# mLSTM with two gated layers on one core: o gates in five pieces, first step's k, q, v ahead of the weights, and a new order for the first third

## The chip, the cores and the metric

The kernel runs on one core of a Trainium2 chip. The metric is the device time of one execution in microseconds (us), the median of several runs; lower is better. The core has TensorE (PE in the rows; its weight loads are PEld), VectorE (DVE), ScalarE (ACT), GpSimd (POOL) and SyncE (SP), which here does nothing but issue loads and stores. Each engine works off its own queue in order and waits on semaphores for the others.

## The reference

```python
def _attn_ref(q, k, v, i_gate, f_gate, o_gate):      # (2, 8, 768, 40), gates without the 40
    for t in range(S):
        m_new = np.maximum(f_gate[:, :, t] + m, i_gate[:, :, t])
        f_stab = np.exp(f_gate[:, :, t] + m - m_new)
        i_stab = np.exp(i_gate[:, :, t] - m_new)
        C = f_stab * C + i_stab * np.einsum('bhd,bhe->bhde', vt, kt)
        n = f_stab * n + i_stab * kt
        h_tilde = np.einsum('bhde,bhe->bhd', C, qt)
        denom = np.maximum(np.abs(np.einsum('bhd,bhd->bh', n, qt)), 1.0)
        y[:, :, t] = sigmoid(o_gate[:, :, t]) * h_tilde / denom

x = y as (1536, 320)
x = (sigmoid(x @ w_gate) * (x @ w_val)) @ w_out      # 320 -> 1536 -> 320
out = ((x @ w_a) * (x @ w_b)) @ w_out2               # 320 -> 1536 -> 320
```

## The kernel before

The recurrence runs in 12 steps of 64 time positions, all 16 heads at once (2 batches, 4 pairs of heads). Within a step it is written with matrices. The layers are cut in 12 blocks of 128 hidden columns each. The weights come as 64-bit floats, are narrowed to 32 bit in the kernel, and each is split into a rounded part and its remainder, since products run in a reduced 32-bit format.

Every piece of work is a task with a name, declared with what it needs and which buffers it takes. The string PLAN lists the tasks in the order in which the kernel issues them; a letter behind a colon picks the engine where there is a choice (V is DVE, G GpSimd, A ACT), and `*n` puts n multiplications by zeros on TensorE ahead of the task. There is no other scheduler: PLAN sets each engine's queue. The names, with s a step, c a block of weights, u a unit:

- loads (SP): `start`, `gl1`, `gl2` the input and forget gates; `cst` constants; `kq`s and `kv`s the keys, queries and values; `og`i the o gates; `w`c weights. Two weight blocks can be held at a time (`wst`, freed by `s2`, `s3`).
- gates: `ga`, `gb`, `gd`, `gc` on DVE, `ge` on ACT, once for each of three pieces of time.
- a step: `pr` or `pl` prepares the operands of the exponents; `E0`, `E1` form the exponents on TensorE, `X0`, `X1` take exp on ACT; `S` is q times k, `P` the product of S and exp on DVE; `k` weighs the keys, `ST` sums the new state on TensorE and `st` copies it on ACT; `O` is the output, `N` and `M` scale and normalise it with the sigmoid of the o gate; `D` copies some columns twice, `T` transposes, `xh` and `xl` split the tokens.
- `sg`i: the sigmoid of load `og`i on ACT, for several steps at once. `yz`, `yi` set up the three buffers Y that hold values and state.
- weights: `na` on ACT, `nb`, `ns`, `nc`, `nd` narrow; `s1` on ACT, `s2`, `s3` split. `s1` of block 3 or 4 waits for the sigmoids whose o gates lie in that block's buffer.
- a unit (one weight block, two or four groups of 128 tokens): `ma`, `mb` the two products of 8 matmuls, `ga_` the activations, `gp`, `gm` the product, `gh_`, `gl_` its split, `mm` the second product, `ev` its evacuation. The first 24 units, the head, take two groups (256 tokens) and form their sigmoid from exp and tanh (L537 to L539), so that ACT needs one table for them and for `X`. The o gates' sigmoid (L339) needs another table. ACT loads a table when the next function is not in the one it has.

In the head, units are put between the steps of the recurrence: unit 0 and 1 work on steps 0 and 1, 2 and 3 on steps 2 and 3, and so on. A head unit takes one of two banks for `ma` and `mb` together, freed by `gp`. Behind the head come units of 512 tokens.

Of the kernel before, what the change touches and what calls it, by code (L numbers as in the profile page):

```python
# [68 lines left out]
pr1:V nb0 yz0 kv0 E01*1 E10*6 gl2 gc1 yz2 ns0 yz1 kv1 X01 X10 ga2 pr2:V yi0:A nc0 k10:V kq0 yi2:A k00:V E11*4
X11 S0 pr3:V w1 kq1 E02 kq2 nd0:V E12 P10 P00 yi1:A k01:G kv2 ST0 st0 na1 X02 og2 S1*10 X12 k11:G k12:G og1  # L70
kq3 gb2 gd2 O0 kv3 ST1 P11 P01 S2*2 pr4:V sg0 nb1 E03 s10 N0 O1*2 P02 P12 st1 s30:G k02:G kq4 ST2 sg2 N1 s20:V
w2 E13 ns1 sg1 M0:G M1:V X03 nc1 k03:G D1 X13 k13:G O2*1 S3 P03 E04 P13 nd1:V E14 D0 kv4 X04 T0*1 X14 T1 st2
xh0 N2 S4 ST3 xl0 pr5:G kq5 P14 xh1 kv5 xl1 O3 s11 s31:G s21:V P04 E15 ma0 N3 M2:V na2 mb0 k04:V ge2 ma1 M3:V
ga_0 mb1 X15 S5 gp0 D3 k14:G st3 nb2 gm0 D2 T2 T3 ga_1 xh2 ns2 gc2 ST4 gh_0 gl_0:G nc2 xh3 O4 st4 kq6 xl2 xl3
nd2:V w3 E05 X05 ma2 mb2 s12 gp1 gm1 pl3 ga_2 ma3 P15 P05 gh_1 k05:G na3 mb3 s22:V gl_1:V s32:V mm0 mm1 kq7
gp2 ma4 mb4 E06 E07 w4 gm2 ga_3 ev0.0:A ev0.1:A nb3 ns3 nc3 nd3:V X06 gh_2 k15:G X07 N4 kv6 S6 gp3 gm3 kv7 E16
s13 P06 ST5 gl_2:G X16 P16 gh_3 gl_3:V O5 pl4 ga_4 S7 st5 E17 mm2 s23:V s33:G gp4 gm4 N5 mm3 X17 ma5 mb5 na4
M5:V k06:G ma6 P07 gh_4 nb4 gl_4:G mb6 O6 ev1.3:A ga_5 P17 ns4 M4:V ev1.2:A k16:V ST6 gp5 gm5 nc4 ma7 D4 T4
ga_6 D5 T5 gh_5 q17:V gp6 gm6 gl_5:G mm4 xh4 xl4 mb7 xh5 xl5 mm5 ga_7 gh_6 nd4:G gp7 ev2.0 N6 s14 k07:G E08
X08 gl_6:G kq8 k17:V gm7 ma8 M6:V st6 w5 mb8 E18 X18 gh_7 ma9 kv8 gl_7:G E19 mb9 ga_8 q18:G ev2.1 mm6 mm7  # L80
q07:V O7 na5 kq9 gp8 ST7 S8 gm8 ga_9 ma10 mb10 ev3.3 ev3.2 N7 M7:V q08:G kv9 D7 nb5 gp9 ma11 gm9 gh_8 X19 E09
P18 gh_9 gl_9:V kv10 mb11 gl_8:G ga_10 gp10 mm8 st7 pl5 k18:G X09 D6 P08 T6 gm10 gh_10 T7 ns5 xh7 xh6 nc5
k08:G mm9 kq10 k19:V ga_11 xl6 O8 gp11 xl7 ST8 gm11 st8 S9 gl_10:G q19:G nd5:V N8 ma12 mm10 gh_11 E110 X110
mb12 ga_12 ma13 mb13 P09 k09:G s34:V P19 gp12 kq11 s15 gm12 gh_12 gl_11:V ga_13 M8:V ma14 s24:V gp13 D8 q09:G
E010 X010 O9 N9 M9:V gm13 ST9 mb14 s25:V mm11 gl_12:G ga_14 ev4.4:A ma15 gp14 gm14 D9 ev4.5:V gh_13 T8 xh8 xl8
T9 mb15 gl_13:G xh9 xl9 mm12 E111 ga_15 X111 q110:V gh_14 w6 ma16 k110:V gl_14:V mm13 mb16 gp15 gm15 ma17
k010:G mm14 na6 nb6 ga_16 E011 ns6 gp16 gh_15 mb17 nc6 ma18 st9 gl_15:V gm16 ga_17 s35:G w7 kv11 X011 nd6:V
gh_16 s16 mm15 gl_16:G S10 q111:G gp17 gm17 gh_17 S11 q010:V P010 ST10 st10 mb18 ga_18 P110 P111 q011:V P011
ev5.6:V gl_17:G O10 ev5.7:A O11 N10 M10:G mm16 mm17 N11 M11:V na7 D10 D11 T10 T11 gp18 gm18 xh10 gh_18 k111:G
nb7 xh11 xl11 xl10 ma19 mb19 ga_19 gp19 gl_18:G mm18 ns7 ma20 gm19 gh_19 mb20 ga_20 gp20 gm20 gh_20 s36:G ma21  # L90
gl_19:G nc7 mb21 ga_21 gp21 gm21 mm19 ma22 gl_20:G s26:V w8 mb22 ev6.8:A nd7:V ma23 ev6.9:A mm20 mb23 ga_22
gp22 gm22 gh_21 gl_21:G ga_23 gp23 ma24 gm23 s17 mm21 gh_22 mb24 gl_22:G gh_23 gl_23:G ga_24 s27:G k011:V mm22
na8 gm24 ma25 ma26 mb25 s37:G mm23 ga_25 w9 gh_24 mb26 ev7.11:V ev7.10:V gl_24 nb8 ga_26 ma27 ns8 nc8 mm24
gm25 nd8:V gh_25 mb27 gm26 gl_25 ga_27 mm25 na9 ma28 gh_26 gl_26 ma29 gm27 gh_27 ga_28 gl_27 mm26 nb9 ga_29
s18 ns9 nc9 mb28 nd9:V mm27 s38:V s19 s28:V ma30 w10 s29:G ev8.1 gm28 gh_28 mb29 gl_28 ev8.0 ga_30 s39:V ma31
w11 gm29 gh_29 gl_29 ma32 ev8.3 ga_31 na10 mb30 mb31 gm30 nb10 ev8.2 ma33 ns10 nc10 mm28 nd10:G mm29 gh_30
na11 gl_30 gm31 mm30 gh_31 ga_32 gl_31 mb32 s110 mm31 s210:G mb33 s310:G ev9.5 ev9.7 gm32 w12 ev9.4 gh_32 ma34
ga_33 gm33 gl_32 mb34 ev9.6 ga_34 nb11 gh_33 ns11 ma35 nc11 nd11:V mm32 s111 ma36 s211:V s311:G mb35 gl_33
ga_35 w13 mm33 gm35 gh_35 na12 gl_35 ma37 gm34 gh_34 mb36 gl_34 ga_36 mb37 ga_37 gm36 mm34 gm37 ma38 mm35 ma39
gh_36 ev10.11 gh_37 gl_36 ev10.9 ga_38 mb39 ev10.8 gl_37 ev10.10 ga_39 nb12 mb38 ns12 mm36 gm38 gm39 nc12 ma40  # L100
nd12:V mb40 na13 mm37 gh_38 nb13 ns13 ma41 gl_38 gh_39 s112 gl_39 nc13 mm38 ga_40 nd13:G ga_41 mm39 s312:G
mb41 ev11.0 gm40 ev11.1 s212:V ma42 gm41 w14 gh_41 mb42 gh_40 gl_40 gl_41 ga_42 ma43 gm42 ev11.2 ev11.3 yt1
# [831 lines left out]
```

## Time and profile before

| | |
|---|---|
| median of 3 runs | 475.48 us (474.09 to 476.25) |
| span of the profiled execution | 478.0 us |
| PE busy | 465.6 us (97%) |
| DVE busy | 295.1 us (62%) |
| ACT busy | 242.5 us (51%) |
| POOL busy | 101.3 us (21%) |
| HBM read, written | 36.71 MB, 1.97 MB |
| multiplications by zeros | 64 |

The profile is of one execution, and its span is 2.5 us above the median of the other runs. The shares are means over a head, in which five engines work on the recurrence and the first units, and a long rest, in which TensorE does the layers. A busy TensorE need not be one at full clock: the granted clock stands in a line or column of its own. The stretch to look at is the first 140 us.

### The profile page before, as it was taken

To read this page: it belongs to the slowest core of one execution; us is meant where nothing else is said; L and a number is where in the kernel's file an instruction comes from. 1 tells how busy PE (TensorE), PEld (TensorE's weight loads), DVE (VectorE), ACT (ScalarE), POOL (GpSimd) and SP (SyncE) were. 2 spreads that over 40 slices of the span, in tenths; PEclk is the share of its full clock that TensorE was granted. 3 is DMA by queue.
4 is the path that set the end of the run, shared out by engine and by line. 5 is a ranking of instruction groups with operands and counts; after the bars stand their busy time and mean duration, and the time that the engine had idled before them with its cause. 6 is when DMAs were issued, how large, how long until landed. Compare 5 with 4: busy or idle time off the path is not lost.

```text
span 478.0 us, 8676 instructions
## 1 busy us (share of the span) xinstructions
PE 465.6 (97%) x3511; PEld 406.2 (85%) x3516; DVE 295.1 (62%) x505; ACT 242.5 (51%) x455; POOL 101.3 (21%) x110
## 2 busy tenths in 40 slices
...
PEclk9969999999999999999999999999999999999998
...
GB/s 226 309 201 240 86 180 224 32 103 183 1 84 84 1 166 0 83 84 1 33 49 84 7 160 0 1 82 138 28 84 82 1 83 1 0 1 20 36 55 55
DMA packets 10454, 39.31 MB, mean 82 GB/s; under 512 B 1840, under 2 KB 3760, under 8 KB 10416
## 3 DMA queue, kind: packets, MB, share of 16 engines
...
q10 hardware_dynamic: 288, 0.33, 0.2%
...
HBM read 36.71 MB, written 1.97 MB: 81 GB/s over the span
## 4 chain that ended last, share of the span: by engine, by line
PE 86%; DVE 6%; ACT 4%; DMA 2%; issue 2%; SPq 0%; DVEq 0%
PE pa L524 30%; PE pb L524 23%; PE acc L531 8%; PE acc L532 8%; PE acc L533 8%; PE o L445 2%; PE sp L416 2%; DMA wst<-in_w_dram 2%; PE st L435 1%; ACT Dt L378 1%; PE e L371 1%; PE t L487 1%; DVE g L556 1%; PE tp L487 1%; PE first L174 1%
## 5 line engine op out<-in xcount | busy, mean ns | idle before, releaser
L524 PE MATMUL pa<-xb,W 128*128 128x512 f32 (+1 forms) x864 | 169.4, 343 | 0.3 <-DVE ge L605 0.3
L524 PEld LDWEIGHTS pa<-xb,W 128*128 128x128 f32 x864 | 136.3, 188 | 18.9 <-DVE ge L605 0.5
L524 PE MATMUL pb<-xb,W 128*128 128x512 f32 x480 | 119.0, 392 | 0.0
L524 PEld LDWEIGHTS pb<-xb,W 128*128 128x128 f32 x480 | 89.0, 188 | 17.9
L560 ACT ACTIVATE gh<-g 128x512 fp32r<-128x512 f32 (+1 forms) x84 | 47.5, 568 | 110.7 <-PE acc L532 55.6
L531 PE MATMUL acc<-W,gh 128*128 128x320 f32 x288 | 89.3, 310 | 0.0
L532 PE MATMUL acc<-W,gh 128*128 128x320 f32 x288 | 88.9, 309 | 0.0
L533 PE MATMUL acc<-W,gl 128*128 128x320 f32 x288 | 88.8, 309 | 0.0
L554 DVE TENSOR_TENSOR g<-g,pb 128x512 f32<-128x512 f32 x60 | 40.9, 685 | 69.7 <-PE pb L524 61.6
L565 DVE TENSOR_TENSOR gl<-g,gh 128x512 fp32r<-128x512 f32 (+1 forms) x66 | 45.5, 694 | 44.0 <-ACT gh L560 43.8
L549 ACT ACTIVATE g<-pa 128x512 f32<-128x512 f32 x60 | 35.6, 595 | 45.8 <-DVE gl L565 38.1
L532 PEld LDWEIGHTS acc<-W,gh 128*128 128x128 f32 x288 | 54.0, 188 | 2.1
L531 PEld LDWEIGHTS acc<-W,gh 128*128 128x128 f32 x288 | 54.0, 188 | 2.0
L533 PEld LDWEIGHTS acc<-W,gl 128*128 128x128 f32 x288 | 54.0, 188 | 0.0
L258 POOL TENSOR_TENSOR W<-wst,W 128x832 fp32r<-128x832 f32 x9 | 19.1, 2124 | 84.5 <-DVE x2tok L639 42.2
L639 DVE SCALAR_TENSOR_TENSOR x2tok<-acc,x2tok 128x320 f32<-128x320 f32 x52 | 23.8, 485 | 19.5 <-PE acc L533 19.5
L242 POOL TENSOR_TENSOR wst<-cva,wst 128x960 int32<-128x960 int32 x7 | 16.9, 2410 | 73.8 <-DVE cva L236 61.1
L218 ACT ACTIVATE cva<-wst 128x960 f32<-128x960 f32 x24 | 25.8, 1077 | 10.6 <-DVE wst L242 8.8
L252 ACT ACTIVATE W<-wst 128x832 fp32r<-128x832 f32 x24 | 23.2, 966 | 11.5 <-DVE wst L242 8.5
L236 DVE SCALAR_TENSOR_TENSOR cva<-wst,cva 128x960 int32<-128x960 int32 x24 | 27.9, 1161 | 0.4
L565 POOL TENSOR_TENSOR gl<-g,gh 128x256 fp32r<-128x256 f32 x18 | 15.7, 876 | 54.7 <-ACT gh L560 47.3
L219 ACT ACTIVATE wst<-wst 128x960 int32<-128x960 uint32 x24 | 26.1, 1087 | 0.0
...
## 6 DMA issues: line engine op xcount, KB each, us to landing
...
cs<-in_cst_dram SPq DMA_DIRECT2D x1, 469.0 KB
rhsE<-V SPq DMA_DIRECT2D x24, 2.0 KB
```

The source lines that it names most:

```text
L218: nc.scalar.activation(cva[0], hi.bitcast(F32), AF.Abs)
L219: nc.scalar.activation(lo, lo.bitcast(U32), AF.Copy, scale=2.0**-29)
L236: nc.vector.scalar_tensor_tensor(ai, hi, -0x40000000, ai, op0=ALU.bitwise_and, op1=ALU.bitwise_or)
L524: nc.tensor.matmul(dst, w[:, w0 : w0 + P], x[:, h, cb], start=(i == 0), stop=(i == 7))
L531: nc.tensor.matmul(a, gh[:, c], wh, start=st, stop=False)
L532: nc.tensor.matmul(a, gh[:, c], wl, start=False, stop=False)
L533: nc.tensor.matmul(a, gl[:, c], wh, start=False, stop=sp)
L549: nc.scalar.activation(t, pa, AF.Copy if l else AF.Sigmoid)
L554: nc.vector.tensor_tensor(t, t, pb, op=ALU.mult)
L560: nc.scalar.activation(gh, g, AF.Copy)
L565: eng.tensor_tensor(gl, g, gh.bitcast(F32), op=ALU.subtract)
L639: nc.vector.scalar_tensor_tensor(dst[:, 0:DM], acc, half, dst[:, 0:DM], op0=ALU.mult, op1=ALU.add)
```

## The change

The o gates come in five loads with five sigmoids (`OGS`) in place of three: steps 0 and 1, 2 and 3, 4 and 5, 6 to 8, 9 to 11. They lie in the buffers of weight blocks 3 and 4, as before. `load_og` finds the place in the buffer by the lowest step in it, since the last piece is now loaded ahead of the fourth. PLAN is rewritten up to `mm21`; from there on it is the same. In the new part 63 multiplications by zeros stand, before 64; the longest row of them is 27, before 37. Engines are changed for some tasks: of the normalisations `M`, GpSimd has 7 in place of 1; of the splits `gl_` DVE has 10 in place of 6; of the head's evacuations DVE has 6 in place of 2, ACT 4 in place of 8.

```diff
-OGS = ((0, 2, 3), (2, 6, 3), (6, 12, 4))
+OGS = ((0, 2, 3), (2, 4, 3), (4, 6, 3), (6, 9, 4), (9, 12, 4))
...
 PLAN = """
-start gl1 cst rhs0:A lhs0:A ga0 ga1 gb0 gd0 ge0 lhs1:A w0 gb1 na0 gc0 gd1 ge1 pr0:V E00*37 og0 X00 rhs1:A
+yz2 start yz0 yz1 gl1 ga0 cst gb0 ga1 lhs0:A gd0 gb1 kv0 kq0 gl2 lhs1:A ge0 rhs0:A gd1 gc0 w0 yi0:A pr0:V
...
-            ogw[k] = wpool.tile([P, 2 * NH + 2 * P], F32, tag=f"W{k}", name=f"og{k}"), s0
+            ogw[k] = wpool.tile([P, 2 * NH + 2 * P], F32, tag=f"W{k}", name=f"og{k}"), min(o[0] for o in OGS if o[2] == k)
```

The loads at the start, on SP's queue. Names end in a running number; kq0 and Y0 are step 0's, wst0 is the first weight block, og3 the o gates in the buffer of block 3. Before:

```order
L678 DMA cs_96<-in_cst_dram 128x938
L211 DMA wst0_135<-in_w1_dram 128x1920
L335 DMA og3_188<-in_ogate_dram 128x640
L324 DMA Y0_103<-in_kv_dram 64x648
L325 DMA Y0_103<-in_kv_dram 64x648
L275 DMA gates2_210<-in_gates_dram 64x2x320
L324 DMA Y1_104<-in_kv_dram 64x648
L325 DMA Y1_104<-in_kv_dram 64x648
L320 DMA kq0_231<-in_kqT_dram 128x1024
L211 DMA wst1_266<-in_w1_dram 128x1920
L320 DMA kq1_268<-in_kqT_dram 128x1024
```

Now:

```order
L679 DMA cs_96<-in_cst_dram 128x938
L325 DMA Y0_103<-in_kv_dram 64x648
L326 DMA Y0_103<-in_kv_dram 64x648
L321 DMA kq0_138<-in_kqT_dram 128x1024
L276 DMA gates2_140<-in_gates_dram 64x2x320
L212 DMA wst0_149<-in_w1_dram 128x1920
L321 DMA kq1_191<-in_kqT_dram 128x1024
L336 DMA og3_199<-in_ogate_dram 128x640
L325 DMA Y1_104<-in_kv_dram 64x648
L326 DMA Y1_104<-in_kv_dram 64x648
L321 DMA kq2_245<-in_kqT_dram 128x1024
```

The k, q, v of step 0 (Y0 and kq0) moved from behind the first weight block and the first o gates to ahead of both; the second weight block, before the twelfth load, is now the sixteenth.

ACT's queue at the first exponentials (Dt is the exp of the exponents e, with the half and the step in its name; L218 and L219 are `na`). Before:

```order
L218 ACTIVATE cva0_139<-wst0_135 128x960
L219 ACTIVATE wst0_135<-wst0_135 128x960
L305 ACTIVATE gates1_116<-gates1_116 64x320
L306 ACTIVATE gates1_116<-gates1_116,cs_96 64x320
L378 ACT_TABLE_LOAD
L378 ACTIVATE Dt0_0_190<-e0_0_186 128x512
L682 ACTIVATE rhsE1_100<-cs_96 128x1024
L378 ACTIVATE Dt0_1_218<-e0_1_200 128x512
L378 ACTIVATE Dt1_0_220<-e1_0_208 128x512
```

Now:

```order
L683 ACTIVATE rhsE0_99<-cs_96 128x1024
L575 ACTIVATE Y0_103<-cs_96 64x8x40 x2
L306 ACTIVATE gates1_119<-gates1_119 64x320
L307 ACTIVATE gates1_119<-gates1_119,cs_96 64x320
L379 ACT_TABLE_LOAD
L379 ACTIVATE Dt1_0_195<-e1_0_182 128x512
L379 ACTIVATE Dt0_0_197<-e0_0_187 128x512
L683 ACTIVATE rhsE1_100<-cs_96 128x1024
L379 ACTIVATE Dt0_1_238<-e0_1_226 128x512
L219 ACTIVATE cva0_240<-wst0_149 128x960
L220 ACTIVATE wst0_149<-wst0_149 128x960
```

`na` of the first block moved from ahead of the first three exponentials to behind them, and the copies into Y0 ahead of them.

ACT's queue around the second batch of sigmoids (x2tok from og; xb is the split of tokens, Y from st the state; a line number of the changed code is one higher). Before:

```order
L457 ACTIVATE Y2_105<-st1_370 40x8x41 x2
L339 ACTIVATE x2tok_97<-og4_308 128x6x320
L339 ACTIVATE x2tok_97<-og3_188 128x4x320
L378 ACT_TABLE_LOAD
L378 ACTIVATE Dt0_3_487<-e0_3_415 128x512
L482 ACTIVATE xt1_472<-xt1_472 128x64
```

Now:

```order
L379 ACTIVATE Dt0_4_524<-e0_4_500 128x512
L340 ACT_TABLE_LOAD
L340 ACTIVATE x2tok_97<-og3_199 128x2x320
L492 ACTIVATE xb0_485<-tp1_532 128x3x128
L458 ACTIVATE Y0_103<-st2_540 40x8x41 x2
L340 ACTIVATE x2tok_97<-og3_199 128x2x320
L340 ACTIVATE x2tok_97<-og4_397 128x3x320
```

Before, the sigmoids of steps 2 to 11 stood ahead of the exponentials of step 3, with one table load behind them; now those of steps 2 to 5 and 9 to 11 stand behind the exponentials of step 4, with a table load ahead and one behind, and the state's and the tokens' copies stand between. A last sigmoid, of steps 6 to 8, stands alone between two more table loads, ahead of the activations of unit 4.

## Rows read from the trace of the kernel before

**Rows 1.** The page: TensorE's busy time, and its granted clock in 40 slices

```profile
PE 465.6 (97%) x3511; PEld 406.2 (85%) x3516; DVE 295.1 (62%) x505; ACT 242.5 (51%) x455; POOL 101.3 (21%) x110
...
PEclk9969999999999999999999999999999999999998
```

**Rows 2.** Windows: stretch, its length, busy time of each engine, granted clock, DMA

```profile
core 0: us, PE busy (x) PEld busy (x) DVE busy (x) ACT busy (x) POOL busy (x), PEclk, DMA share, GB/s
0.00:5.99 5.99, 4.82 (x12) 1.80 (x13) 2.74 (x10) 1.49 (x3) 3.60 (x7) 1.00 0.57 169
5.99:52.53 46.54, 41.75 (x625) 29.58 (x629) 37.60 (x75) 38.76 (x69) 11.57 (x16) 0.89 0.82 248
52.53:66.87 14.34, 14.34 (x223) 13.20 (x219) 13.48 (x25) 12.84 (x29) 5.08 (x7) 1.00 0.46 155
27.57:37.80 10.23, 9.49 (x129) 7.02 (x133) 4.81 (x13) 6.90 (x11) 3.31 (x6) 0.50 0.41 101
24.00:27.57 3.57, 2.08 (x68) 1.80 (x62) 3.46 (x7) 3.52 (x6) 0.74 (x1) 1.00 1.01 391
45.40:478.00 432.60, 426.18 (x3000) 381.52 (x2998) 261.44 (x436) 209.25 (x403) 87.86 (x90) 1.00 0.20 65
...
73.00:103.00 30.00, 29.01 (x401) 27.75 (x397) 26.94 (x53) 22.04 (x54) 16.05 (x14) 1.00 0.42 124
```

**Rows 3.** Waits of PE, 45.4 to 140 us: us in total, times, longest

```profile
PE st L435 <- DVE Kw L381: 0.7, 1, 0.7
PE pa L524 <- DVE ge L605: 0.3, 1, 0.3
```

**Rows 4.** Waits of ACT, 5.9 to 67 us, the three that count

```profile
ACT xt L482 <- DVE xt L477: 3.2, 1, 3.2
ACT Dt L378 <- PE e L371: 2.3, 2, 1.9
ACT cva L218 <- DMA wst<-in_w_dram: 1.7, 1, 1.7
```

**Rows 5.** Timeline (start, us, engine, line, operation) of PE: ma2, mb2, ma3, mb3

```profile
53.44 3.94 PE L524 MATMUL pa<-xb,W 128*128 128x256 f32 x32
```

**Rows 6.** Timeline of ACT; in brackets the idle time before and its releaser

```profile
5.99 1.06 ACT L682 ACTIVATE rhsE<-cs 128x1024 fp32r<-128x1024 f32 x1 [3.77 <-DMA cs<-in_cst_dram]
...
24.04 1.09 ACT L378 ACTIVATE Dt<-e 128x512 f32<-128x512 f32 x2
25.14 1.28 ACT L339 ACT_TABLE_LOAD   x1
26.44 0.74 ACT L339 ACTIVATE x2tok<-og 128x640 f32<-128x640 f32 x1
...
29.52 2.96 ACT L339 ACTIVATE x2tok<-og 128x1920 f32<-128x1920 f32 x2
...
50.35 0.39 ACT L537 ACTIVATE ge<-pa 128x256 f32<-128x256 f32 x1
...
51.37 0.47 ACT L491 ACTIVATE xb<-tp 128x384 fp32r<-128x384 f32 x1
51.74 0.41 ACT L560 ACTIVATE gh<-g 128x256 fp32r<-128x256 f32 x1
52.05 0.48 ACT L491 ACTIVATE xb<-tp 128x384 fp32r<-128x384 f32 x1
```

**Rows 7.** Windows, columns as in rows 2: the loads' pace

```profile
6.00:9.00 3.00, 3.00 (x13) 1.19 (x11) 2.81 (x9) 2.69 (x5) 0.00 (x0) 1.00 0.98 348
9.00:12.00 3.00, 3.00 (x16) 1.42 (x14) 2.88 (x6) 1.62 (x2) 0.00 (x0) 1.00 1.04 224
```

**Rows 8.** Timeline of SP's queue: two loads that follow each other

```profile
7.45 0.58 SPq L320 DMA_DIRECT2D kq<-in_kqT_dram  x1
10.38 0.33 SPq L211 DMA_DIRECT2D wst<-in_w_dram  x1
```

**Rows 9.** Timeline of PE: ma5, mb5, ma6, mb6

```profile
68.18 3.93 PE L524 MATMUL pa<-xb,W 128*128 128x256 f32 x32
```

More of the change, by code (lines that the diff above doesn't have):

```diff
@@ L67 @@
 PLAN = """
-start gl1 cst rhs0:A lhs0:A ga0 ga1 gb0 gd0 ge0 lhs1:A w0 gb1 na0 gc0 gd1 ge1 pr0:V E00*37 og0 X00 rhs1:A
[L69 to L102, printed above, removed]
@@ new lines @@
+E10*27 E00*3 pr1:V kq1 ge1 X10 X00 og0 ga2 gc1 S0 P00 E01 E11*2 kv1 P10 gb2 rhs1:A X01 na0 yi1:A kq2 pr3:V
+pr4:G k00:V X11 nb0 O0*9 yi2:A pr2:V k11:G kv2 S1 E02 P11 P01 w1 S2*3 E12 ns0 k10:G kq3 ST0 k01:V nc0 kq4 sg0
+X02 E03 nd0:V N0 X12 og1 st0 og2 kv3 gd2 E13*6 s10 og4 ST1 O1*1 P12 k02:V M0:G X03 s30:G X13 D0 P02 s20:V N1
+T0 E14 S3*1 na1 st1 M1:V xh0 k12:G P13 ge2 pr5:G xl0 nb1 ns1 nc1 gc2 E04*2 O2*2 D1 X14 X04 P03 nd1:G sg1 T1*3
+w2 xh1 xl1 ST2 st2 sg2 N2 S4 k03:V sg4 kv4 M2:G s11 P14 D2 kq5 P04 O3*2 ma0 na2 N3 M3:V E05 E15*2 mb0 s21:V
```

78 lines of the change are left out of this document (54 added, 24 removed).

## Prediction

> **What bounds the kernel now.** I read the page first: TensorE is busy 465.6 of 478.0 us, and the line of granted clocks is full but for slices early and at the very end [rows 1]. Then I cut the span. From 45.4 us, where the first matmul of the experts (ma0) starts, TensorE is busy 426.18 of 432.60 us, nearly all of the rest at the end; up to 140 us its waits are 0.7 and 0.3 us [rows 2, 3]. From 45.4 us on it is thus a full pipe, and only the head of 45 us can give time back. The head has small waits of TensorE, a stretch of 10.23 us at half clock (27.57 to 37.80, granted 0.50, behind 3.57 us in which TensorE was busy for 2.08), and many multiplications by zeros [rows 2]. In it ACT and DVE do the recurrence's exponentials and products and the narrowing of the weights: from 5.99 to 52.53 us ACT is busy 38.76 of 46.54 us and DVE 37.60 [rows 2]. ACT's idle 7.78 us has names: 3.2 us for the normalised tokens, 2.3 for exponents, both inside or just behind the half-clock stretch, and 1.7 for the first weights [rows 4].
>
> So the head is a race of ACT, DVE and TensorE, and what counts is when TensorE gets to a point behind which it is never hungry, with the same work behind it.
>
> **The change, as a sum.** I take as that point the first matmul of unit 2 (ma2, steps 2 and 3). Before, it starts at 53.44 us [rows 5]. Both orders put the same TensorE work ahead of it (exponents of steps 0 to 5, S0 to S5, ST and O 0 to 4, four transposes, units 0 and 1), with 64 zeros' matmuls before and 63 now. A lead at ma2 is a lead at the end if TensorE stays fed.
>
> *What ma2 waits for.* The last input is the token split of step 3: xh3 on ACT, ended at 52.53 us, then a subtraction on DVE; ma2 came 0.91 us behind xh3 [rows 5, 6]. What must ACT do ahead of xh3 in the new order? The old 38.76 us, and
> - two more table loads, 2 x 1.28 = +2.57 (the first sigmoid now stands between exponentials, and three more stand alone later) [rows 6];
> - one exponential that stood later (X05): +0.5, half of a pair of 1.09 [rows 6];
> - the sigmoids: 0.74 and 2.96 = 3.70 before; now three of two steps, 3 x 0.74, and one of three steps, 1.0 by the slope between those rows: 3.2, so -0.5 [rows 6];
> - unit 1's three activations go behind it, 51.37 - 50.35 = -1.0, and a copy of unit 0, 52.05 - 51.74 = -0.3 [rows 6].
>
> That is 40.0 us. The constants still land third, so ACT starts at 5.99, and without a wait xh3 ends at 46.0 and ma2 starts at 46.9: a lead of 6.5 us.
>
> *Do the others keep up?* DVE has the same sum of work ahead of its last subtraction (a narrowing step, a preparation and three small products go to GpSimd or behind; another narrowing step, a split and four small products come in): from 5.99 us on, its 37.60 us and 0.6 for that subtraction end at 44.2. GpSimd gets some 3 us more there and was busy 11.57 of 46.54 us [rows 2]. TensorE: it was busy 4.82 + 41.75 us up to 52.53 and all of the 0.91 us to 53.44; less 4.7 us of slowness (half of the 9.49 us busy at half clock) and 0.2 for one zeros' matmul that is 42.5 us, from 1.17 us (5.99 - 4.82) on, so 43.7 us [rows 2, 5]. ACT is the longest of the three, and DVE is close to it.
>
> *Waits of ACT that stay.* The first step's k, q, v now go in ahead of w0. The loads move 1.02 MB by 6 us, 2.06 MB by 9 us and 2.73 MB by 12 us (169, 348 and 224 GB/s) [rows 2, 7]. By the shapes, at 4 bytes, the k, q, v of step 0 end at 1.57 MB, so at some 8 us and the landing, and S0 needs them at about 12. w0 ends at 2.71 MB, about 11.9 us; before, it ended at 1.69 MB, 7.9 us by the same account, and had landed at 10.38, 2.5 us later [rows 7, 8]. So it lands near 14.4 us. ACT comes to it (gates, copies, one table load, exponentials, a copy of 1.0) near 14.7. This is nearly a tie, and na0 stands in ACT's queue ahead of the state's identities, the third exponential and the first sigmoid, so a late w0 is passed on in full. SP gains: before, it stood still after kq0 (issued 7.45) until w0 had landed, and issued the next load at 10.38; now eight loads lie between w0 and the first one that waits for it [rows 8]. Before, ACT's idle time without the three named waits was 0.65 us. I take 2.0 us of waits in all: 0.5 for w0, and 1.5 for the places where ACT and DVE hand over to each other with under 1 us to spare. The ends: 0, and the 7.78 us of before. So ma2 at 48.9, a lead of 4.5 us (ends 6.5 and -1.3).
>
> *Behind ma2.* Another sigmoid with a table load on each side stands ahead of unit 4's activations. From xh3 to there ACT was busy 12.84 us (52.53 to 66.87) [rows 2]. Now it is +2.57 for loads, +1.0 sigmoid, +1.3 for unit 1 and the copy above, +1.6 for recurrence work that stands earlier, -1.5 for work that moves to DVE or behind: 17.85. From 48.0 us that ends at 65.9, and the clip adds 0.5: 66.4. Unit 6's first matmul waits for that bank. Before, it ran third in its row, at 68.18 + 1.89 = 70.07 us [rows 9]; with the lead and 1.15 us more of recurrence ahead of it, TensorE would come to it at 70.07 - 4.5 + 1.15 = 66.7. ACT is 0.3 us early: a tie again. I charge 0.5 us (ends 0 and 3.6, the sigmoid and both loads in full). Further on ACT has 22.04 busy of 30 us [rows 2], so it should not bind again. The order from mm21 on is word for word the old one.
>
> The sum: 6.5 - 2.0 - 0.5 = **4.0 us less**. The profiled span is 478.0 and the median of the runs 475.48; I take the difference over: 475.48 - 4.0 = **471.5 us**.
>
> **A rule against the row.** Four more table loads are the dearest thing that the change adds. In the trace the load at 25.14 begins when the exponentials end (24.04 + 1.09), and the sigmoid begins at 26.44: 1.3 us, all in [rows 6]. The Trainium skill (ScalarE: Activation LUTs, What ACT_TABLE_LOAD costs) gives 1283 ns for the load, as here, and some 1380 ns more of drain for every switch. By it two loads ahead of ma2 would cost 2.8 us more and the time would be 474.3 us. The row shows no drain, and 1.3 us stands.
>
> **The rivals.** *TensorE's clock falls again.* The new order spreads 63 zeros' matmuls thinly, 27 ahead of the first exponent and then one to nine at a time, and TensorE is filled to 42.5 of 47.7 us up to ma2. Before, 3.57 us with 1.5 us of waiting and no zeros in them went ahead of the fall. One stretch as before takes 4.7 us, of which half of TensorE's 5.2 us of slack takes up 2.6: 2.1 us lost, **473.6 us** (471.5 to 476.2). For it: gaps of about 1 us remain around the second table load and ahead of step 4's exponents. Against it: zeros stand at each gap.
>
> *Slower: the clock stays down through two such stretches.* The place is 15 to 45 us. The price is 2 x 4.7 less 2.6 of slack: 6.8 us, 471.5 + 6.8 = **478.3 us**. It decides the sign when more than some 13 us of the head run at half clock (4.0 + 2.6 us lost). For it: ACT would then wait for TensorE, which makes TensorE sparser still. Against it: in the old order it recovered after one.
>
> *ACT waits as much as before.* If its idle time is not w0's and the clock's but a property of the hand-overs, the lead at ma2 is -1.3 and the time **476.8 us**, no change. For it: DVE has hardly more room than ACT. Against it: 7.1 of the 7.78 us stand in three waits with causes that go [rows 4].
>
> *The early loads do not come early.* If w0 lands 2 us later than ACT gets to it, in place of 0.5, it is 1.5 us: 473.0 us.
>
> **How the numbers follow.** The forecast with its own range (469.0 to 473.1) has 0.60. One fall of the clock has 0.14, ACT's waits 0.10, a late w0 0.03, the skill's drain 0.02, two stretches 0.11. About 0.5% (2.4 us) is what a measurement can tell from no change: under 473.1 is faster, over 477.9 slower. With the halves of the clock's case and the late w0 on the fast side, faster has 0.66, same 0.22, slower 0.12. The range reaches from the full lead (469.0, and a little for the runs' own scatter) to past ACT's case: 468.5 to 477.0.
>
> **What would show it.** Right: the first exponential near 12.5 us, w0 waited for under 1 us, ACT without a wait of 3 us up to xh3, ma2 near 49 us, full clock or one short fall in the head, TensorE with under 1 us of waits from there to 80 us, and the same time from mm21 on. Wrong: a clock of 0.50 for over 10 us between 15 and 45 (clock rivals); many waits of 0.3 to 1 us on ACT from DVE (ACT's rival); TensorE idle for the bank around 65 us (the second sigmoid pair); a table load with a gap behind it (the drain).

## The result, and the profile after

The changed kernel takes **478.47 us** (median of 19 runs, 476.80 to 481.94) where the kernel before takes 475.48 (19 runs): a ratio of 1.0059, 95% interval 1.0034 to 1.0085. It is slower by 0.6%; the forecast was 471.5 us and faster. The time also lies above the forecast's range (468.5 to 477.0).

The profiled execution of the changed kernel has a span of 475.7 us, and so is 2.3 us *shorter* than the profiled one of before (478.0). Between the two profiles the change looks like a gain, between the medians like a loss. TensorE's granted clock falls to half for another length of time from one execution to the next of the same kernel. The device time is the span plus some 1.8 us in most executions (up to 3.3 us in a few).

The page of the changed kernel (compare [rows 1]):

```profile
PE 464.7 (98%) x3509; PEld 405.0 (85%) x3515; DVE 296.3 (62%) x504; ACT 246.0 (52%) x457; POOL 112.2 (24%) x121
...
PEclk9999999999999999999999999999999999999999
```

Its windows, columns as in [rows 2]: from the constants' landing to the end of xh3, from there to unit 4's activations, a stretch ahead of the clock's fall, the fall, from 45.4 us to the end:

```profile
5.98:49.84 43.86, 38.83 (x603) 27.54 (x609) 39.27 (x74) 39.83 (x69) 14.44 (x16) 0.96 0.78 241
49.84:67.74 17.90, 17.90 (x315) 16.48 (x311) 15.46 (x31) 17.50 (x36) 11.86 (x15) 1.00 0.58 183
30.00:33.63 3.63, 1.60 (x10) 0.60 (x7) 3.56 (x6) 2.97 (x9) 1.50 (x2) 1.00 0.95 328
33.63:37.04 3.41, 3.08 (x36) 2.30 (x36) 2.21 (x3) 2.45 (x3) 2.02 (x1) 0.50 0.75 209
45.40:475.70 430.30, 425.53 (x3005) 379.57 (x3003) 257.50 (x426) 208.99 (x397) 94.14 (x98) 1.00 0.21 68
```

The waits of TensorE and ACT in the head (compare [rows 3, 4]; from 45.4 to 140 us the view of TensorE's waits has no row any more):

```profile
PE e L372 <- DVE lhsE L352: 2.1, 2, 1.2
PE e L372 <- ACT Dt L379: 2.0, 1, 2.0
```

```profile
ACT xb L492 <- PE tp L488: 1.5, 1, 1.5
ACT Dt L379 <- PE e L372: 0.6, 1, 0.6
```

The timeline of TensorE at ma2 (compare [rows 5]):

```profile
50.70 1.21 PE L525 MATMUL pa<-xb,W 128*128 128x256 f32 x8
```

TensorE's timeline at step 4's first exponent, with the two zeros' matmuls ahead of it:

```profile
30.29 0.61 PE L175 MATMUL first<-zb 128*128 128x512 bf16 x2
32.93 0.50 PE L372 MATMUL e<-rhsE,lhsE 128*128 128x512 f32 x1 [2.03 <-ACT Dt L379]
```

ACT's timeline at the last sigmoid, its two table loads and unit 4's activation:

```profile
63.02 1.28 ACT L340 ACT_TABLE_LOAD   x1
64.31 1.01 ACT L340 ACTIVATE x2tok<-og 128x960 f32<-128x960 f32 x1
65.33 1.28 ACT L538 ACT_TABLE_LOAD   x1
66.63 0.38 ACT L538 ACTIVATE ge<-pa 128x256 f32<-128x256 f32 x1
```

What to see: ACT is busy 39.83 us up to xh3 (forecast 40.0), of its three long waits [rows 4] 0.6 us for exponents are left in this view and a new one of 1.5 us stands at the tokens (xb), and TensorE waits nowhere behind ma2. In 30.00 to 33.63 us TensorE is busy 1.60 of 3.63 us, with one wait of 2.0 us for step 4's first exponential, and then the clock is at 0.50 for 3.41 us. ma2 comes at 50.70.

### The profile page after: what moved, and what is told of

It reads as the page before. It is cut to its first block, busy times and chain, and to the rows that moved or that the text cites. A ratio compares the mean times of both kernels' runs of the same rounds, so it can differ in the third digit from the quotient of the medians.

```text
span 475.7 us, 8703 instructions
## 1 busy us (share of the span) xinstructions
PE 464.7 (98%) x3509; PEld 405.0 (85%) x3515; DVE 296.3 (62%) x504; ACT 246.0 (52%) x457; POOL 112.2 (24%) x121
## 4 chain that ended last, share of the span: by engine, by line
PE 92%; ACT 5%; DMA 1%; issue 1%; DVE 0%; SPq 0%
PE pa L525 33%; PE pb L525 23%; PE acc L532 9%; PE acc L533 9%; PE acc L534 9%; PE o L446 2%; PE sp L417 2%; PE st L436 1%; DMA cs<-in_cst_dram 1%; ACT Dt L379 1%; PE e L372 1%; PE tp L488 1%; PE t L488 1%; ACT Y L575 1%; ACT L379 1%
## 5 line engine op out<-in xcount | busy, mean ns | idle before, releaser
L525 PE MATMUL pa<-xb,W 128*128 128x512 f32 (+1 forms) x864 | 172.0, 344 | 0.0
L566 DVE TENSOR_TENSOR gl<-g,gh 128x512 fp32r<-128x512 f32 (+1 forms) x70 | 48.4, 696 | 44.3 <-ACT gh L561 44.2
L259 POOL TENSOR_TENSOR W<-wst,W 128x832 fp32r<-128x832 f32 x11 | 23.6, 2145 | 84.4 <-DVE x2tok L640 42.2
L219 ACT ACTIVATE cva<-wst 128x960 f32<-128x960 f32 x24 | 26.0, 1082 | 8.9 <-DVE wst L243 8.8
L566 POOL TENSOR_TENSOR gl<-g,gh 128x256 fp32r<-128x256 f32 x14 | 12.1, 869 | 38.3 <-ACT gh L561 36.3
```

The costliest lines, as they stand in the source:

```text
L219: nc.scalar.activation(cva[0], hi.bitcast(F32), AF.Abs)
L525: nc.tensor.matmul(dst, w[:, w0 : w0 + P], x[:, h, cb], start=(i == 0), stop=(i == 7))
L566: eng.tensor_tensor(gl, g, gh.bitcast(F32), op=ALU.subtract)
```

## The experiments

In each table row the span is the median over executions whose mean granted clock is above 0.996; their number stands behind it. I call these executions without a fall, since the shortest fall seen, 3.41 us at half clock, takes the mean clock of a 474 us span down to 0.996 by itself. (At 0.996 and under an execution may also owe it to the last few us, which are at half clock in every profile.) Kernels of one heading ran on one chip (h3 alone on another), beside the kernel before.

### First question: what was the profiled execution of before?

**e1**: the kernel before, unchanged, profiled again.

> The kernel before, unchanged, to see how its executions spread. Theory A: the profiled execution of before (span 478.0, mean granted clock 0.986, 10.2 us of its head at half clock) was one of its slow ones; its usual execution keeps the clock (mean 0.995 or more) and has a span of some 473 to 474 us, and a new profile shows ma2 near 49 to 50 us in place of 53.4. Theory B: its clock is 0.986 in most executions, span about 478, and the 2.3 us that the two profiles differ by are lost elsewhere. A: median span under 475 with clock 0.99 or more. B: median span 477 to 478.

Measured: 475.70 us, ratio 1.0019 (0.9989 to 1.0049). The clock fell again, for 6.8 us in place of 10.23. Windows of e1, ahead of the fall and in it:

```profile
25.00:29.20 4.20, 2.66 (x85) 2.06 (x83) 3.44 (x9) 4.12 (x7) 1.24 (x3) 1.00 1.03 340
29.20:36.00 6.80, 6.78 (x95) 4.92 (x87) 3.11 (x7) 5.50 (x6) 3.11 (x5) 0.50 0.42 110
```

ma2 stands at 52.19 us in e1 (53.44 in [rows 5]), the span is 476.7. Of the 35 timed executions of before on this chip 20 had no fall, with a median span of 472.5 us; only one was at a clock as low as the profiled one's (0.986), with 477.5. Over all chips 14 of the 143 timed executions of before are at 0.987 or under. So the profile that the prediction was worked out from shows an unusually long fall. Theory A holds for the timed executions (median span 473.9 us in e1); the new profile did not show the head without a fall that it was to give.

**e2**: the kernel before, with step 0's k, q, v loaded first, and nothing else of the change.

```diff
-... yz0 kv0 E01*1 ... nc0 k10:V kq0 yi2:A
+yz0 start gl1 cst kv0 kq0 rhs0:A ...
```

> The old order with one thing changed: the first step's k, q, v are loaded ahead of the first weights. In the old queue of ACT the first weights' narrowing stands ahead of the first exponentials, so whatever they land later is waited for. Theory A (the new order is slow by its own head, not by its loads): the wait for w0 grows from 1.7 us to 4 to 5, and the time is 1 to 3 us longer than before; in the new order that wait is gone. Theory B (the early loads are a cost of their own there too): more than 4 us longer.

Measured: 476.59 us, ratio 1.0041 (1.0016 to 1.0067): slower, 1.7 us by the medians, with 473.7 us in 3 of 12 executions without a fall (before 472.5). The wait for w0 was expected to grow to 4 to 5 us and has 2.4 (the row's 2.8 are two waits):

```profile
ACT cva L218 <- DMA wst<-in_w_dram: 2.8, 2, 2.4
```

[rows 4] had 1.7 us, but the profiles of the old order with its loads unmoved (e1, f2, f4, g3, g4) have 0.7 to 2.9, so this one row does not show that the wait grew. In after `na0` stands behind the first exponentials, and ACT does not wait for w0 at all. Shown is that the early loads bring nothing by themselves in the old order; that they cost by way of w0 is argued.

**e3**: the changed kernel with pr5 (a preparation on GpSimd) two steps later. In the trace of after, DVE's normalisation M1 ran beside it. The rows of DVE and of GpSimd (two views of one stretch):

```profile
29.71 1.55 DVE L478 SCALAR_TENSOR_TENSOR xt<-nrm,xt 128x320 f32<-128x320 f32 x1
```

```profile
29.66 1.25 POOL L346 TENSOR_TENSOR rhsE<-V,cs 32x512 fp32r<-32x512 f32 x1
```

```diff
-... P13 ge2 pr5:G xl0 ... xh1 xl1 ...
+... P13 ge2 xl0 ... xh1 pr5:G xl1 ...
```

> The new order with one task moved on GpSimd: the preparation of step 5 (pr5, 1.25 us) runs behind the narrowing of the second weight block in place of ahead of it. In the profile of the changed kernel the normalisation M1 on DVE took 1.55 us instead of 0.49 while pr5 ran, the split xl0 came 1 us later, step 4's exponent waited 2.0 us on TensorE, and the clock fell at 33.6 us. Theory A: M1 is back at 0.5 us, TensorE's wait of 2.0 us shrinks to about 1, the clock falls in fewer executions, and the time is 1.5 to 3 us shorter than the changed kernel's (475.5 to 477). Rival (the long M1 has nothing to do with pr5): M1 stays at 1.5, time as the changed kernel's, 478.5.

Measured: 477.05 us, ratio 1.0052 (1.0024 to 1.0080), as after within the intervals; one of 12 executions is without a fall. M1 is at 0.49 us again, and TensorE still waits, and the clock still falls, at 33.0 us for 3.41. DVE's and TensorE's rows of e3:

```profile
29.34 0.49 DVE L478 SCALAR_TENSOR_TENSOR xt<-nrm,xt 128x320 f32<-128x320 f32 x1
```

```profile
32.24 0.50 PE L372 MATMUL e<-rhsE,lhsE 128*128 128x512 f32 x1 [1.93 <-ACT Dt L379]
```

The slow M1 is real and costs 1.06 us on DVE, but it is not what makes TensorE wait or the clock fall. That idea of mine fell.

**e4**: the changed kernel with nine zeros' matmuls in place of two ahead of step 4's exponent, in that wait.

```diff
-E04*2 O2*2 D1
+E04*9 O2*2 D1
```

> The new order with nine multiplications by zeros ahead of step 4's exponent in place of two: they fill the 2.0 us wait of TensorE with work that nobody needs. Theory A (the fall of the clock is what costs): the clock holds in the head, the mean clock is 0.995 or more in most executions, and the time is 1 to 2.5 us shorter than the changed kernel's 478.5, though the wait itself stays. Rival (the wait costs and the clock does not): same time as the changed kernel, or 0.5 us longer.

Measured: 475.66 us, ratio 1.0033 (0.9998 to 1.0069). 8 of 12 executions are without a fall; of the changed kernel's 19 none is. Its windows and its ma2:

```profile
5.90:47.90 42.00, 39.93 (x616) 27.38 (x615) 39.55 (x74) 40.03 (x69) 14.81 (x16) 1.00 0.81 252
30.00:33.63 3.63, 3.20 (x21) 1.30 (x22) 3.56 (x6) 2.98 (x7) 1.37 (x2) 1.00 1.00 343
33.63:37.04 3.41, 3.41 (x99) 2.83 (x97) 2.95 (x6) 3.08 (x6) 2.15 (x1) 1.00 0.66 195
```

```profile
48.76 1.21 PE L525 MATMUL pa<-xb,W 128*128 128x256 f32 x8
```

This is the forecast's head almost to the tenth: ACT busy 40.03 of 42.00 us up to xh3 (forecast 40.0 and 2.0 of waits), ma2 at 48.76 (forecast 48.9). The fall had cost 50.70 - 48.76 = 1.9 us (1.5 against 49.23 in the profile of h2, the same kernel again). And yet the span without a fall is 473.6 us where before's executions without a fall have 472.5. So even at full clock the new order, with these seven zeros, is some 1.1 us behind.

### Second question: what does the new order lose behind ma2?

From ma2 on all kernels have the same 2859 matmuls of TensorE. Summed from each start to the next they take 418.05 us in e2 (old order) and 419.89 in e4 (new order), though e4's TensorE never waits there (e2's waits 0.3 us). What differs is how often TensorE goes from the recurrence's pieces (S, ST, O, T) to the rest (E, ma, mb, mm) and back: 24 borders in the old order, 48 in the new.

**f1**: e4 with its pieces of the recurrence moved together, eleven tasks of TensorE by one or two places.

```diff
-... ma4 S7 mb4 S6 T4 ma5 ST6 mm2 ... S9 mb8 S8 ma9 ... T7 ma10 T6 ...
+... ma4 mb4 S7 S6 T4 ST6 ma5 mm2 ... S9 S8 mb8 ma9 ... T7 T6 ma10 ...
```

> The kernel e4 with eleven of TensorE's tasks moved by one or two places between ma2 and mm21, so that pieces of the recurrence (S, ST, O, T) stand together: 26 borders between them and the rest (E, ma, mb, mm), where e4 has 48 and the old order 24. Theory B (a border costs TensorE time that no wait shows): from ma2 to the end the same 2859 matmuls take 418.05 us in e2's trace with 24 borders and 419.89 in e4's with 48, counted from each start to the next: 0.08 us a border, so 22 borders less give 1.7 us: ma2 to the end 423.2 us in place of 424.9, a span of 471.9 us at full clock (e4 473.6), and the device time 1.7 us under e4's. Theory C (the loss behind ma2 comes from ACT's extra sigmoids and table loads or from GpSimd's extra products): nothing, 424.9 and 473.6. A rival to B: the moved tasks now wait for their inputs or hold up others, and waits of TensorE of 1 to 2 us appear behind ma2.

**f2**: the kernel before with zeros in the 1.5 us in which its TensorE stood still at 26 us.

```diff
-ST1 P11 P01 S2*2
+ST1*7 P11 P01 S2*4
```

> The kernel before with nine more multiplications by zeros: seven ahead of ST1 and four in place of two ahead of S2, at the 1.5 us in which TensorE stands still at 26 us. Theory A (the profiled execution of before was a slow one because the clock fell behind this gap; at full clock the old order is as good as the new): no stretch at half clock in the trace, or a short one; ma2 at 48.0 to 48.7 us, where the two traces of before have 53.4 and 52.2; a span of 472.4 us; full clock in more than half of the executions (12 of 35 of before), so a median of 474.2 us, 0.5 to 1 us under before. Rival: the clock falls for another reason than the gap, as often and as long as before: 475 us, and ma2 at 50 us or later.

**f3**: e4 with og3's sigmoid beside og4's, which takes two table loads away.

```diff
-... T1*3 w2 ... sg4 kv4 ... mb3 og3 ... P06 sg3 gl_2:V
+... T1*3 og3 w2 ... sg4 sg3 kv4 ... mb3 ... P06 gl_2:V
```

> The kernel e4 with the fourth o gates' load moved ahead of w2 and their sigmoid next to the one of the fifth, so that the last two table loads go (ACT 2.57 us less ahead of unit 4's activations, 1.0 us more ahead of unit 1's). Theory B: TensorE has no wait behind ma2 in e4's trace, so nothing is gained there: a span of 473.6 us at full clock, up to 0.5 more if the sigmoid delays ma2. Theory C (these loads cost time behind ma2, the 0.5 us of the prediction and up to its end of 3.6): 0.5 to 2.6 us less, 471.0 to 473.1.

**f4**: f2 with five tasks of TensorE moved behind ma2, 18 borders (in this diff, as in those of f1 and g4, only TensorE's tasks are shown).

```diff
-... E07 S6 E16 ... ma7 T4 T5 ... mm8 T6 T7 mm9 ...
+... E07 E16 S6 ... T4 T5 ma7 ... mm8 mm9 T6 T7 ...
```

> The kernel f2 (old order with nine more zeros) with five of TensorE's tasks moved by one or two places behind ma2: 18 borders between recurrence and the rest, where the old order has 24. Theory B: six borders by 0.08 us, 0.5 us under f2, ma2 to the end 423.4 us if no wait appears. Theory C: the same as f2. Either is near what can be told apart by time alone; the trace from ma2 to the end decides.

| | device time | ratio (interval) | span without a fall |
|---|---|---|---|
| before | 476.33 | | 473.6 (11 of 35) |
| f1 | 477.14 | 1.0008 (0.9985 to 1.0030) | 474.0 (5 of 12) |
| f2 | 477.65 | 1.0016 (0.9985 to 1.0047) | 474.4 (6 of 12) |
| f3 | 476.61 | 1.0019 (0.9995 to 1.0042) | 474.6 (9 of 12) |
| f4 | 477.88 | 1.0041 (1.0013 to 1.0069) | 474.8 (7 of 12) |

f4's profile is the one that e1 was to give: the old order's head at full clock (up to ma2 it is the kernel before with nine more zeros). Its windows, its ACT waits, and ma2:

```profile
5.99:48.00 42.01, 38.71 (x631) 27.11 (x635) 38.49 (x76) 38.80 (x69) 13.09 (x16) 1.00 0.88 274
24.00:27.57 3.57, 3.41 (x67) 2.21 (x65) 3.36 (x8) 3.52 (x6) 0.76 (x2) 1.00 1.03 349
```

```profile
ACT Dt L378 <- PE e L371: 1.0, 1, 1.0
ACT cva L218 <- DMA wst<-in_w_dram: 0.7, 1, 0.7
ACT xt L482 <- DVE xt L477: 0.4, 1, 0.4
```

```profile
48.85 3.94 PE L524 MATMUL pa<-xb,W 128*128 128x256 f32 x32
```

The three waits of [rows 4] that add up to 7.2 us are 2.1 us here, in the old order, with nothing of the change. ma2 is at 48.85, against 48.62 to 49.23 in the four profiles of the new head with e4's zeros (h1, h3, e4, h2). **At full clock the old head and the new one reach ma2 at about the same time.** One execution does not decide more: g3, the old order again without a fall, came to ma2 at 50.61, behind a wait of 2.2 us for w0 and 1.3 us for the tokens. As an estimate, before's executions without a fall (472.5 us) less the 423.7 to 424.5 us from ma2 to the end of the span in e2 and before put ma2 at 48.0 to 48.8.

f2's own profile was hit by a fall elsewhere, of 6.8 us: at 17.7 us, behind a stretch in which TensorE stood for 2.2 us until the first exponentials came. Its window:

```profile
13.90:17.60 3.70, 1.39 (x6) 0.50 (x6) 3.05 (x6) 3.67 (x6) 0.00 (x0) 1.00 1.01 337
```

So zeros at one gap do not hold the clock when there is another gap ahead of it; the time of f2 is that of before, and not the 474.2 us expected. f4 is slower than before, by an interval clear of 1, and without a fall f2 and f4 are 0.8 and 1.2 us longer than before. Whether that is the price of their nine zeros was not tested. f3 shows that the two table loads and the sigmoid ahead of unit 4 cost nothing behind ma2 (419.93 us from ma2 on, as in after), as theory B had it. The sigmoid's 1.0 us ahead of ma2 may cost up to 0.8 us there: ma2 at 49.3 us (e4 48.76, h2 49.23), with this row in TensorE's waits that e4 does not have:

```profile
PE tp L488 <- ACT Dt L379: 0.8, 1, 0.8
```

f1's grouping won 1.1 us of TensorE's time behind ma2 and gave it back: 420.22 us, of which 1.4 us are waits that e4 does not have; this is the rival to B. Its profile also has a fall of 10.2 us ahead of ma2. f4's six borders less won nothing: 417.8 us without its waits, where f2 has 417.7.

### Third question: is it the borders, and can they be had for nothing?

**g1** is f1 and **g2** is e4, both with `E02*6` in place of `E02`; **g3** is f2 with `E10*10` in place of `E10*6`; **g4** is g3 with its recurrence's pieces moved *apart* behind ma2, eleven tasks by one or two places:

```diff
-... ST5 O5 S7 E17 mm2 ... mb6 O6 ST6 ... O7 ST7 S8 ma10 mb10 ma11 ...
+... ST5 S7 E17 O5 mm2 ... O6 mb6 ST6 ... O7 ma10 ST7 mb10 S8 ma11 ...
```

> The kernel f1 (new order, E04*9, TensorE's pieces of the recurrence grouped: 26 borders) with five more zeros ahead of the exponents of step 2 (E02*6), where f1's TensorE waited 1.3 us for DVE and the clock fell. Beside g2, which has the same zeros and 48 borders, only the grouping differs. Theory B (0.08 us a border): 1 to 1.8 us under g2 in executions at full clock, a span of 472 to 473 us, ma2 to the end 423.2 to 424 us. Rival (the grouped order waits, as in f1's trace, whatever the clock does): the same as g2 within 0.5 us. Clock: full in more than half of the executions, if gaps are what makes it fall.

> The kernel e4 (new order, E04*9, 48 borders) with E02*6. Theory B: ma2 to the end 424.9 us as in e4, no wait of TensorE behind ma2, a span of 473.6 to 474.3 us at full clock, 1.2 us above the fast executions of before on the same chip. Theory on the clock: ma2 at 48.8 to 49.6 us; full clock in at least 7 of 12 executions, more often than in e4.

> The kernel f2 (old order, ST1*7, S2*4) with four more zeros ahead of E10 (10 in place of 6), where TensorE waits 1.1 to 2.4 us for the first exponentials and the first weights, and behind which f2's clock fell at 17.7 us. If it is this gap: full clock in more than half of the executions, ma2 at 48.5 to 49.5 us, a span of 472.5 to 474 us, a median 0.5 to 1 us under before. Rival (the falls of the old order do not hang on the gaps that zeros fill): 8 of 35 at full clock as before, and the time of before.

> The kernel g3 with eleven of TensorE's tasks behind ma2 moved by one or two places so that the pieces of the recurrence stand apart: 46 borders in place of 24. Theory B: ma2 to the end 1.8 us longer than in g3 (22 times 0.08), without a wait of TensorE that would explain it, and the time 1.8 us above g3's in executions of the same clock. Theory C (borders cost nothing by themselves): as g3 within 0.3 us, or longer by waits that the trace names.

| | device time | ratio (interval) | span without a fall |
|---|---|---|---|
| before | 476.61 | | 473.3 (11 of 35) |
| g1 | 476.43 | 1.0011 (0.9980 to 1.0043) | 474.4 (9 of 12) |
| g2 | 476.88 | 1.0018 (0.9984 to 1.0051) | 474.1 (6 of 12) |
| g3 | 476.26 | 0.9995 (0.9961 to 1.0029) | 474.4 (11 of 12) |
| g4 | 478.64 | 1.0032 (1.0000 to 1.0064) | 476.8 (9 of 12) |

g4 against g3 is the clean test, and it came out as expected (1.8 us): 2.4 us slower, by the medians and by the spans without a fall, and from ma2 on 419.8 against 417.8 us when each one's waits are taken off. The same tasks stand in both timelines of TensorE. In g3 O7, ST7 and S8 run in a row, followed by ma10, mb10 and ma11:

```profile
82.64 1.13 PE L445 MATMUL o<-Y,Z 128*64 128x41 f32 x32
83.59 0.79 PE L435 MATMUL st<-Y,Kw 128*40 128x41 f32 x32
84.31 1.15 PE L416 MATMUL sp<-kq 40*64 40x64 f32 x32
85.39 3.10 PE L524 MATMUL pa<-xb,W 128*128 128x256 f32 x24
88.33 0.39 PE L371 MATMUL e<-rhsE,lhsE 128*128 128x512 f32 x1
```

In g4 the products stand between the pieces:

```profile
84.17 1.13 PE L445 MATMUL o<-Y,Z 128*64 128x41 f32 x32
85.23 1.21 PE L524 MATMUL pa<-xb,W 128*128 128x256 f32 x8
86.37 0.81 PE L435 MATMUL st<-Y,Kw 128*40 128x41 f32 x32
87.12 1.21 PE L524 MATMUL pa<-xb,W 128*128 128x256 f32 x8
88.25 1.15 PE L416 MATMUL sp<-kq 40*64 40x64 f32 x32
89.33 1.21 PE L524 MATMUL pa<-xb,W 128*128 128x256 f32 x8
90.38 0.39 PE L371 MATMUL e<-rhsE,lhsE 128*128 128x512 f32 x1
```

From O7 to the E behind ma11 is 88.33 - 82.64 = 5.69 us in g3 and 90.38 - 84.17 = 6.21 in g4, for the same matmuls, with no idle time in either. What changes at a border is the field behind MATMUL, the active rows and columns of the array (its tile, for short): 128*64, 128*40 and 40*64 for O, ST and S, 128*128 for the units. Counted by that field (which I did only after these runs), the changes between 128*128 and the smaller tiles behind ma2 order the kernels:

| | such changes | ma2 to the end, waits taken off |
|---|---|---|
| f4 | 14 | 417.8 |
| old order: before, e1, e2, f2, g3 | 16 | 417.8, 418.0, 417.8, 417.7, 417.8 |
| old order behind the new head: h3 | 16 | 418.6 |
| f1, g1 | 24 | 418.8, 418.9 |
| g4 | 30 | 419.8 |
| new order: after, e3, e4, f3, g2, h2 | 36 | 419.8 to 419.9 |

From 16 to 30 and to 36 that is 0.14 and 0.11 us a change, at 24 it is 0.13; in the rows of g3 and g4 above, which have no transposes, four changes more cost 0.52 us, 0.13 each. It is in TensorE's busy time, so that no view of waits shows it. h3 lies 0.8 us above the others of 16 (its waits of under 0.15 us are not in the view), so a single value is good to some tenths. g4 against g3 shows that the order alone costs; that it is the change of tile is argued from this count. Two things do not fit it cleanly: borders with transposes, 128*128 too, have about 0.1 us in some rows, and there are 16 of them in g4, 14 in the new order and 8 in the old; and an S behind an O or an ST comes after 1.03 and 0.72 us, nearly as late as a product (1.06, 0.72 to 0.74), though both are small. The Trainium skill (TensorEngine Tiling (Array Packing), Key Properties) says that a change of the tiling mode drains TensorE; the page gives no figure, and whether these borders are such changes no run here shows.

g3 held the clock, 11 of 12 against 11 of 35, but not the time: its span without a fall is 1.1 us *longer* than before's. Why is open. In its profile E10 started at 15.8 us (f4 14.4), but not for the four zeros more: they end at 14.8, and TensorE waits on for ACT, which had waited 2.2 us for w0 (0.7 in f4).

```profile
15.82 0.51 PE L371 MATMUL e<-rhsE,lhsE 128*128 128x512 f32 x1 [1.06 <-ACT Dt L378]
```

g2's profile had a fall from 10.7 to 20.9 us, behind 3.1 us of waiting for the gates, with this window ahead of it:

```profile
7.00:10.70 3.70, 1.49 (x7) 0.49 (x5) 3.40 (x8) 3.31 (x7) 0.00 (x0) 1.00 1.09 254
```

g1 against g2, the grouping alone: +0.3 us at full clock, -0.45 in the medians, no difference clear of noise, as the rival expected (theory B: 1 to 1.8 us less). It saves 1.0 us of changes and has 1.3 us of new waits behind ma2:

```profile
PE pa L524 <- DVE ge L605: 0.6, 1, 0.6
PE sp L416 <- ACT Dt L378: 0.4, 1, 0.4
PE tp L487 <- DVE Z L426: 0.3, 1, 0.3
```

### Fourth question: the new head with the old order behind it

**h1**: e4 up to ma2, from there the old order of all tasks that are left (og3 ahead of kq6, sg3 ahead of ga_4). **h2**: e4 again. **h3**: h1 with og3 loaded behind kv7 and sg3 ahead of ga_5.

```diff
-... ST4 N4 og3 st4 kq6 ma2 ... gp3 gm3 kv7 E16 ... pl4 sg3 ga_4 ... ga_5
+... ST4 N4 st4 kq6 ma2 ... gp3 gm3 kv7 og3 E16 ... pl4 ga_4 ... sg3 ga_5
```

> The new order with E04*9 up to ma2, and from there on the old order of all that is left (the o gates' load og3 and its sigmoid sg3 kept, ahead of ma2's row and ahead of ga_4): 24 borders behind ma2 in place of 48. In g4 and g3, 22 borders more cost 2.0 us behind ma2 once the waits are taken off (419.8 against 417.8); in f1 and g1 the grouping of the new order won 1 to 1.4 us, and new waits of 1.3 to 1.4 us took it back. Theory B (the borders are what the new order loses behind ma2): ma2 at 48.8 us as in e4, ma2 to the end 423.0 to 423.5 us if the old order's waits of 0.3 us stay the only ones, 471.8 to 472.3 us at full clock, 1.5 us under e4 in the same job. Rival (the new head hands over its work in a state in which the old order waits, since more of the units' activations are still to come on ACT): 473.6 us as e4, with waits of TensorE for ACT or DVE of 1 us and more behind ma2.

> The kernel e4 once more, beside the hybrid on the same chip: 473.6 us at full clock, in some 8 of 12 executions, ma2 to the end 424.9 us.

> The hybrid h1 with og3 loaded behind kv7 in place of ahead of kq6, and its sigmoid ahead of ga_5 in place of ga_4. In h1's trace TensorE stood still for 1.7 us in the middle of S7 (at 61.2 us, no releaser in the trace) while the loads moved over 400 GB/s, and the clock fell behind it for 3.4 us; with that wait and the fall taken off, h1's TensorE needs 417.7 us from ma2 on, as the old order does, and e4 419.9. If the moved load takes the crowd away: no wait of TensorE over 0.6 us behind ma2, no fall, ma2 to the end 423.0 to 423.5, a span of 471.8 to 472.5 us at full clock, 1.2 us under before's executions at full clock. Rival: the wait in S7 stays wherever the load stands, and the time is h1's, 475.6 to 477 us of span.

Measured: h1 479.06 us, ratio 1.0081 (1.0046 to 1.0116), one of 11 executions without a fall. h2 475.74 us, 0.9985 (0.9957 to 1.0013), 473.9 us in 11 of 12; before had 476.15, and 473.1 us in 7 of 21. h3, on another chip, 477.90 us, 1.0053 (1.0025 to 1.0080), 474.8 us in 5 of 12; before had 476.17 there, and 472.9 us in 6 of 17. Both hybrids are slower than before, where they were expected to be faster. The hybrids' TensorE has the old number of changes. But h1 stood for 1.7 us in the middle of S7, with nothing in the trace that releases it, and the clock fell behind it; in h3 that wait is gone and another of 1.6 us stands a little later. In h1's stop itself (61.24 to 62.94 us) the loads move 113 GB/s, not the 400 of the expectation, so that h3 does not show a crowd of loads to be the cause. The row of h1's timeline and the one of h3's waits:

```profile
62.94 0.45 PE L416 MATMUL sp<-kq 40*64 40x64 f32 x7 [1.70 <-issue]
```

```profile
PE pa L524 <- DVE ge L605: 1.9, 2, 1.6
```

So 1 to 2 us behind ma2 can be taken off TensorE, and in f1, g1, h1 and h3 they came back as waits. No kernel here beats the one before by more than the intervals: the nearest are h2 (0.9985) and g3 (0.9995).

## Why the prediction was wrong, step by step

**The step that failed** is the last one: "The profiled span is 478.0 and the median of the runs 475.48; I take the difference over". The sum itself ends at a span of 478.0 - 4.0 = 474.0 us, and e4, the new order without a fall, has 473.6. But the 4.0 us were worked out against an execution in which the clock had been down for 10.23 us, and were subtracted from a median of executions most of which had no such stretch (129 of 143 are above 0.987). A span of 478.0 is 479.8 us of device time, so the profile stood 4.3 us above the median, not 2.5. Taken as an absolute time, the walk says 474.0 + 1.8 = 475.8: no change. The sign came from the subtraction. Of the 7.0 us between 471.5 and 478.47 it is 4.3; the other 2.7 are about what falls of the clock add to the changed kernel's median (below).

**What bounds the kernel** was read wrongly in one place. "7.1 of the 7.78 us stand in three waits with causes that go" used causes that for the most part go by themselves: f4, in the old order, has 2.1 us in the same three rows. Two of them, 5.5 us, stood in or behind the half-clock stretch and are 1.4 in f4; the third, 1.7 us for w0, came ahead of the fall and differs from profile to profile of the old order (0.7 to 2.9). The 4.7 us that I counted as TensorE's slowness were what the lead at ma2 consisted of: 53.44 - 48.85 = 4.6 us goes with the clock (and nine zeros, and 1.0 us less of waiting for w0) in the old order, and 48.85 - 48.76 = 0.1 is the change's.

**The walk through the new head was right.** First exponential 12.98 us (forecast near 12.5), no wait for w0 (0.5), ACT 39.83 to 40.03 us busy (40.0), waits of 2.0 us in e4 (2.0), ma2 at 48.8 there (48.9). From xh3 to unit 4's activations ACT was busy 17.50 us (forecast 17.85; the terms add up to 17.81). No drain is seen at a table load: in the rows above the sigmoid begins 0.01 us behind the load's end, and the next load 0.01 us behind the sigmoid's. By the rule of the Trainium skill (ScalarE: Activation LUTs, What ACT_TABLE_LOAD costs) some 1.4 us would lie at each switch; the measurement decides against it here.

**The clock rival happened** inside the loss: one fall in after, priced at 2.1 us, measured 1.9 (50.70 against 48.76). It was given 0.14; none of the changed kernel's 19 executions had a mean clock above 0.996, where 20 of 35 of before's had beside the first experiments. The rival with two stretches named 478.3 us, next to the measured 478.47, but that is luck: it takes some 13 us at half clock, and the changed kernel's median execution has a mean clock of 0.992, that of e1's profile with its 6.8 us. "Zeros stand at each gap" was wrong for step 4's exponent: two of them end at 30.9 us and the exponent comes at 32.93. Seven zeros more there were worth 2.8 us in the median (478.47 to 475.66), of which 0.6 is the difference of the two medians of before beside them (475.48 and 474.85); the ratios' intervals overlap (1.0034 to 1.0085, 0.9998 to 1.0069). The counts without a fall are clear: 0 of 19 in after, 1 of 12 in e3, 8 of 12 in e4.

**Behind ma2** I charged 0.5 us for the second sigmoid pair. That mechanism is not there: no wait at ga_4 in after, nothing gained in f3. What is there are 20 more changes of tile, 2.1 us, of which I had no term; the old order's 1.0 us of waits that are gone [rows 3] and 0.6 us less from the last matmul to the end (4.8 against 5.4, not looked into) take off most of it, so that the two profiles differ from ma2 on by only 425.0 - 424.5 = 0.5 us. That it is just what I charged is luck, and no support. The tile fields 128*40, 128*64 and 40*64 were in the trace of before, and a part of the price could be read there: from an ST to an O behind it 0.64 us, to a unit's product 0.72 to 0.74. In the rows of g3 and g4 it is 0.95 us from an O to an ST, 1.06 to a product.

**Put together**, in spans: without a fall the new order is 1.1 us (e4 to before, first chip) or 0.8 us (h2, later chip) behind; the falls add 476.5 - 473.6 = 2.9 us to the changed kernel's median and 473.1 - 472.5 = 0.6 to before's. 1.1 + 2.9 - 0.6 = 3.4 us; the medians of the result differ by 3.0. The terms come from different chips, and 0.4 us is within what these differ by.
